# One core, one long program: the same steps in another order on every engine

## The chip, the cores and the metric

The kernel runs on one core of a Trainium2 chip. A core has engines with an instruction queue each, which run side by side and wait for one another by semaphores: TensorE (PE in the profile; PEld are its weight loads), VectorE (DVE), ScalarE (ACT), GpSimd (POOL) and SyncE (SP), which here issues all transfers between the chip's memory and the core's own memory (SBUF). TensorE writes its results to PSUM, eight banks of 2 KB per partition. The metric is the time of one run on the device, in microseconds (us), as the median of several runs; lower is better.

## The reference

A gated linear attention, computed token by token, is followed by a feed-forward block with a hard-swish.

```python
def _attn_ref(q, k, v, alpha):            # each (4, 8, 768, 48)
    state = np.zeros((B, H, D, D), dtype=np.float32)
    for t in range(S):
        state = alpha[:, :, t, :, None] * state + np.einsum('bhd,bhe->bhde', k[:, :, t], v[:, :, t])
        y[:, :, t] = np.einsum('bhd,bhde->bhe', q[:, :, t], state)

def _moe_ref(x, w_in, w_out):             # x (3072, 384), w_in (384, 2048), w_out (2048, 384)
    h = x @ w_in
    g = h * np.clip(h + 3.0, 0.0, 6.0) / 6.0
    return g @ w_out
```

x is the attention's output with batch and sequence as rows and heads times 48 as columns. The weights come as 64-bit floats and the kernel rounds them itself.

## The kernel before

The 3072 tokens are worked on as 24 chunks of 128 (index j), six for each of the four batch entries, and the feed-forward block as 12 groups of two chunks (index g). Everything is unrolled: the program is a list of 1788 words such as `ta.0.0`, and each word emits the few instructions of one step. The name ahead of the first point is the step, the numbers are the chunk or group, a part, and the buffer or PSUM bank that is used. As each engine runs its queue in order, the list is at the same time the order of every engine's queue, and of SyncE's transfers. No scheduler changes it (`tc.manual_schedule()`); the framework only puts in the semaphores.

The steps, by their names in the list, with the line that shows in the profile and the engine:

- Loads on SyncE: `la`, `lk`, `lq` bring alpha, k and q of a chunk (L251 for chunks 0 to 5, one transfer; L262 from chunk 6 on, four transfers into tiles in blocks of 32, with two small memsets on GpSimd, L257, for chunks 6 and 7). `lv` brings v in two halves (L272). `w.i` brings slice i of the weights (L162 for the eight slices of w_in, L166 for the eight of w_out) into one of five buffers, of which slices 0 and 5, 1 and 6, 2 and 7 and so on share one.
- Rounding a weight slice: ScalarE takes the low half (`d1`, L186), the magnitude (`d2`, L196) and, for slices 0, 1, 2 and 4, the sign (`dx`, L191, 1.9 us); VectorE puts the high bits together (`d3`, L203 and L205, or L207, L208 and L210); GpSimd adds both (`d4`, L217). Slice i of w_in is needed by block i of the first product, slices 8+2p and 9+2p of w_out by part p of `b`.
- Attention of a chunk: `ta`, `tk`, `tq` turn alpha, k and q on TensorE (L282) for chunks 0 to 5; later chunks are turned by VectorE (L286). `ca` copies alpha (L300, ScalarE), `r` scans it backwards and inverts (L309, L313), `p` scans it forwards (L320), `k` and `q` multiply by the scans (L332, all VectorE). `sc` makes the scores (L346, TensorE), `m` masks them (L356, VectorE), `qa` copies q (L366, ScalarE). `kb` turns k back (L374) and `ck` copies it (L378, ScalarE); from chunk 8 on `kt`, `kw`, `kr` do that by VectorE and two trips through memory. `u` updates the state (L429, TensorE), `sm` adds it (L437, L439, VectorE), `st` decays it (L409, GpSimd), `sv` copies it (L419, ScalarE; L415, a memset on GpSimd, at the start of a batch entry). `ya` and `yb` make the two halves of the output (L455, TensorE), `cy` copies it to x (L464, ScalarE).
- Feed-forward of groups 0 and 1: `fa`, `fb` (halves, L489) and `f` (L478) are the first product, `fr` (L494, ScalarE) and `fg` (L498, VectorE) the gate, `b` (L516) the second product for the two chunks of group 0, `bo` and `so` copy and store it.
- Feed-forward of groups 2 to 11: a fast bilinear scheme with 20 small products for 24. `y` (L537 to L541, VectorE) makes sums of weight blocks once, `xc` sums of x blocks for each group, `M.g.i` is product i (L600, TensorE), `n` copies some products (L606, ScalarE), `o` sums them (VectorE), `e` and `h` are the gate (L494, L498).
- Second product of groups 1 to 11, by a Strassen-like scheme: `x` (L647) sums weights once, `s` (L647, L664) sums the gated block (VectorE), `P.g.i` is product i (L703, TensorE), `K` and part 3 of `G` copy (L682, L716, ScalarE), the other `G` add (L719, VectorE), `O` stores (L724, SyncE). The four buffers of `G` are named by the last number.
- `z.m.n` is a filler: n matmuls of the identity into bank m (L532) that nobody reads.

The words begin with the fillers and the first chunk, and the step table and the loop that runs them are the whole control:

```python
    def run(words):
        for word in words.split():
            name, *at = word.split(".")
            steps[name](*(int(x) for x in at))
```

Of the kernel before, what the change touches and what calls it, by code (L numbers as in the profile page):

```python
# [17 lines left out]
def kernel(  # L18
# [42 lines left out]
    G = 2  # L61
# [510 lines left out]
    for i in range(8):  # L572
        r, o = divmod(i, 3)
        spots.append(raws[r].rearrange("p n w -> p (n w)").bitcast(FP)[:, o * QB : (o + 1) * QB])
    xc = consts.tile([C, len(X_SUMS), C], FP, tag="xc")
# [174 lines left out]
    with tc.manual_schedule():  # L750
        run("""z.0.5 z.0.3 z.0.1 z.0.8 qa.0.0 w.0 d2.0 d3.0 la.0 ta.0.0 ca.0 r.0 lk.0 tk.0.1 k.0
               z.0.2 p.0 la.1 ta.1.2 lq.0 tq.0.3 ca.1 r.1 lk.1 lv.0.0 sv.0.0 d1.0 kb.0.0 ck.0 z.0.2
               u.0.2.1 sm.0.0 sv.0.1 q.0 qa.0.1 tk.1.0 k.1 p.1 z.0.2 sc.0.2.3 m.0 la.2 ta.2.0 ca.2
               dx.0 w.2 d2.2 kb.1.0 ck.1 lq.1 r.2 sm.0.1 st.1 tq.1.2 q.1 d3.2 z.0.3 d1.2 dx.2 lv.1.1
               u.1.3.1 sv.1.0 sm.1.0 p.2 sm.1.1 sc.1.0.2 m.1 ya.0.3 yb.0 cy.0 lq.2 w.1 d1.1 tq.2.1
               q.2 d4.2 lk.2 tk.2.3 k.2 fa.2.0 d4.0 st.2 sc.2.0.2 d2.1 d3.1 m.2 dx.1 d4.1 qa.1.1
               lk.3 la.3 ta.3.1 ca.3 la.4 fa.0.1 sv.1.1 w.3 r.3 ta.4.3 ca.4 r.4 tk.3.1 k.3 kb.2.0
               qa.1.0 d2.3 ya.1.2 yb.1 cy.1 fa.1.2 lq.3 ck.2 d1.3 p.3 d3.3 lv.2.2 u.2.3.2 sm.2.0
               d4.3 fb.2 tq.3.1 q.3 fb.1 qa.2.0 sm.2.1 sv.2.0 st.3 fr.0.2.0 fg.0.2 lk.4 tk.4.0
               sv.2.1 w.5 d2.5 k.4 d3.5 d1.5 qa.3.0 d4.5 qa.2.1 sc.3.1.3 m.3 w.6 d2.6 d1.6 d3.6 d4.6  # L760
               lv.3.0 lq.4 w.7 kb.3.2 fb.0 f.0.3.3 kb.4.0 ya.2.1 ck.3 u.3.3.2 sm.3.0 fr.0.3.1 fg.0.3
               fr.0.1.0 fg.0.1 qa.3.1 sv.3.0 sm.3.1 p.4 d2.7 sv.3.1 d1.7 d3.7 d4.7 f.0.5.0 fr.0.5.1
               fr.0.0.0 fg.0.5 fg.0.0 tq.4.3 ck.4 la.5 ta.5.2 f.0.6.3 ca.5 w.4 d2.4 ya.3.0 yb.3 cy.3
               fr.0.6.1 yb.2 cy.2 w.9 d2.9 q.4 qa.4.1 d1.4 d1.9 dx.4 la.6 w.8 d3.4 r.5 lk.5 w.10
               d3.9 p.5 ca.6 fg.0.6 d4.9 w.12 lq.5 lv.4.1 d2.8 d3.8 f.0.7.2 d1.8 st.4 d4.8 d4.4 w.11
               fr.0.7.0 fg.0.7 f.1.7.0 fr.1.7.1 fg.1.7 sc.4.0.2 m.4 f.1.1.1 fr.1.1.0 fg.1.1 f.1.3.3
               fr.1.3.1 d2.10 d1.10 tk.5.3 f.1.0.2 d2.12 d3.10 d4.10 w.13 fg.1.3 fr.1.0.0 fg.1.0 k.5
               d3.12 lq.6 f.1.6.0 f.1.2.1 u.4.1.0 sm.4.0 d1.12 d4.12 sv.4.0 qa.4.0 ya.4.2 fr.1.6.1
               fg.1.6 w.15 tq.5.3 fa.4.3 sv.4.1 d2.11 kb.5.1 d2.13 fr.1.2.0 f.1.4.2 fr.1.4.1 d1.11
               sm.4.1 q.5 r.6 d3.11 d3.13 fg.1.4 d4.11 lv.5.0 lk.6 tq.6 p.6 d2.15 d3.15 fg.1.2 d1.13  # L770
               d4.13 sc.5.0.3 yb.4 f.1.5.0 fr.1.5.1 fg.1.5 tk.6 m.5 b.1.0.2 fb.4 b.1.1 d1.15 d4.15
               st.5 y.5 w.14 la.7 lk.7 cy.4 d2.14 qa.5.1 ck.5 b.0.0.1 fr.0.4.0 d3.14 k.6 q.6 ca.7
               fg.0.4 d1.14 d4.14 x.0 y.1 y.10 b.0.1 y.0 y.2 u.5.2 P.1.0.0 K.1.0 qa.5.0 sv.5.0
               qa.6.1 P.1.1.3 b.0.2 b.1.2 kb.6.0 ya.5.3 y.6 s.1.0.0 sm.5.0 sv.5.1 G.1.0.0 tk.7
               s.1.1.1 s.1.2.3 x.1 yb.5 cy.5 b.1.3 sc.6.1.2 lv.6.2 ck.6 u.6.3.0 s.1.3.2 x.2 P.1.2
               b.0.3 K.1.1 y.7 s.1.4 s.1.5 y.11 y.3 r.7 xc.2.1 x.3 y.4 y.8 xc.2.3 k.7 xc.2.0 xc.2.4
               y.9 y.12 y.16 y.13 y.15 P.1.3.3 K.1.2 P.1.4 bo.1 P.1.5 xc.2.5 G.1.1.1 P.1.6 y.14 y.17
               y.19 xc.2.6 sm.6.0 G.1.2.2 y.20 M.2.0.2 lv.12.1 la.8 O.1.1 O.1.0 ca.8 y.18 y.21 y.23
               so.1 G.1.3.3 n.2.0.8 bo.0 lq.7 lv.7.0 O.1.2 m.6 xc.2.2 xc.2.10 xc.2.7 tq.7 r.8 p.7
               xc.2.8 sv.6.1 M.2.15.3 M.2.1 kb.7.3 n.2.1.9 M.2.16 M.2.2 n.2.2.10 M.2.7.0 n.2.7.11  # L780
               sm.6.1 xc.2.9 q.7 p.8 M.2.3 M.2.4 n.2.4.12 M.2.8 o.2.0.0 M.2.5 n.2.5.13 qa.7.0 sv.6.0
               st.7 lk.8 O.1.3 lq.8 lk.9 la.9 la.10 tk.8 tq.8 lq.10 lq.9 ya.6.1 yb.6 M.2.9 z.1.3
               M.2.18.1 o.2.1.0 e.2.1.1 M.2.10 cy.6 ck.7 sc.7.0.2 u.7.1.3 n.2.10.14 M.2.11 qa.7.1
               ca.9 la.11 y.22 M.2.6.2 h.2.1 q.8 m.7 e.2.0.0 h.2.0 n.2.11.15 qa.6.0 n.2.18.10 qa.8.1
               M.2.12 M.2.19 n.2.12.12 M.2.13 sm.7.0 sv.7.1 r.9 k.8 o.2.3.0 sv.7.0 ya.7.0 y.24
               o.2.5.0 n.2.13.12 o.2.2.0 yb.7 cy.7 sc.8.1.2 xc.3.1 o.2.2.1 e.2.2.1 xc.3.3 o.2.3.1
               M.2.14 xc.3.4 xc.3.0 xc.3.5 o.2.4.0 xc.3.7 xc.3.6 o.2.6.0 P.2.0.1 M.3.0.2 M.2.17
               h.2.2 o.2.6.1 e.2.3.0 h.2.3 o.2.7.0 K.2.0 n.3.0.12 M.3.1 n.3.1.9 e.2.5.1 M.3.7.0
               n.3.7.13 xc.3.8 o.2.7.1 xc.3.2 kt.8 e.2.6.0 h.2.6 tk.9 M.3.2 n.3.2.10 e.2.4.0 P.2.1.3
               h.2.4 h.2.5 s.2.0.14 e.2.7.0 G.2.0.1 h.2.7 M.3.3 M.3.4 n.3.4.8 k.9 s.2.1.11 M.3.8  # L790
               o.3.0.0 ca.10 kt.9 P.2.3.3 s.2.2.15 s.2.3.14 lv.8.2 kw.8 kr.8 lk.10 sm.7.1 xc.3.9
               M.3.5 n.3.5.11 K.2.2 e.3.0.1 xc.3.10 M.3.9 o.3.1.0 P.2.2 K.2.1 u.8.0.3 M.3.18.2 s.2.5
               M.3.10 n.3.10.14 n.3.18.15 e.3.1.0 s.2.4 P.2.4 tq.9 h.3.0 st.8 sv.8.0 M.3.11 n.3.11.8
               tk.10 p.9 sm.8.0 q.9 r.10 k.10 qa.9.0 qa.9.1 m.8 sm.8.1 h.3.1 M.3.19 o.3.5.0 kt.10
               P.2.5 G.2.2.0 st.9 M.3.12 sc.9.0.1 qa.8.0 n.3.12.10 o.3.3.0 kw.9 lv.9.0 kr.9 sv.8.1
               u.9.2.3 sm.9.0 sv.9.1 sv.9.0 G.2.1.2 sm.9.1 st.10 M.3.15.2 M.3.16 M.3.6.3 M.3.13 m.9
               o.3.4.0 o.3.6.0 tq.10 n.3.13.10 o.3.2.0 e.3.4.1 ya.8.2 yb.8 ya.9.3 yb.9 cy.9 M.3.14
# [135 lines left out]
```

## Time and profile before

| | us |
|---|---|
| median of 3 runs | 535.52 (535.26 to 536.1) |
| the profiled execution | 535.44 |
| its span, first to last instruction | 533.7 |
| TensorE busy | 524.6 |
| VectorE busy | 477.2 |
| ScalarE busy | 257.2 |
| GpSimd busy | 50.4 |
| GpSimd's 16 steps `d4` (L217), 0 to 95 us | 26.9 |

Busy time is the union of an engine's instructions; an engine may be busy and yet not at its best pace, and TensorE's instructions overlap. In a row of the timeline the columns are start, duration, engine, line, operation, result and operands, how many instructions are merged, and in brackets the idle time ahead of it with the instruction that ended it. What the profile calls the chain that ended last gives TensorE 85% of the span and VectorE 8%, nearly all of the latter between 80 and 128 us.

### The profile page before, as it was taken

The numbers are of one execution on the slowest core, as the hardware profiler recorded it, in microseconds if no ns is written. First come the engines' busy times: TensorE is split into PE (matmuls) and PEld (weight loads), VectorE is DVE, ScalarE is ACT, GpSimd is POOL, SyncE is SP. The second block draws the span as 40 slices with busy tenths as digits, with TensorE's granted clock in tenths as the row PEclk, the third lists the DMA queues.
The fourth block names the chain that finished last, engine by engine and source line by source line (L and its number), as shares of the span: only waits on it lengthen the run. The fifth ranks groups of instructions, "written<-read, shape, count | busy, mean of one in ns | idle before, by whom it ended". The sixth has DMA issues, their size and how long they took to land.

```text
span 533.7 us, 15143 instructions
## 1 busy us (share of the span) xinstructions
PE 524.6 (98%) x6306; PEld 499.4 (94%) x6306; DVE 477.2 (89%) x849; ACT 257.2 (48%) x503; POOL 50.4 (9%) x71
## 2 busy tenths in 40 slices
PE   8799999999999999999999999999999999999997
PEld 7698886789999999999999999999999999999997
DVE  6999989999999999998999999999999899496382
ACT  3889865212653553553544444642634544553340
POOL 5333425100000000000000000000000000000000
DMA  9998876005615155254344355044454042100001
GB/s 174 217 252 256 215 216 152 21 2 154 152 30 116 32 121 135 57 140 95 87 110 113 91 124 140 19 120 102 115 136 104 11 110 43 44 2 2 15 16 37
DMA packets 124100, 54.40 MB, mean 102 GB/s; under 512 B 83328, under 2 KB 116864, under 8 KB 124032
## 3 DMA queue, kind: packets, MB, share of 16 engines
q1 hardware_dynamic: 124032, 53.44, 42.5%
q8 instruction: 49, 0.80, 0.6%
q14 instruction: 19, 0.16, 0.1%
HBM read 44.50 MB, written 8.91 MB: 100 GB/s over the span
## 4 chain that ended last, share of the span: by engine, by line
PE 85%; DVE 8%; POOL 2%; DMA 2%; ACT 1%; issue 1%; SPq 1%; DVEq 0%; POOLq 0%
PE m_ps L703 34%; PE m_ps L600 34%; PE m_ps L478 5%; PE t_ps L455 4%; PE t_ps L346 2%; PE t_ps L429 2%; PE m_ps L489 2%; PE t_ps L282 1%; DVE rings L647 1%; DMA v<-in_v_dram 1%; DVE raw L537 1%; ACT raw L191 1%; DMA kq<-in_k_dram 1%; DVE g_sb L647 1%; DVE w L537 1%
## 5 line engine op out<-in xcount | busy, mean ns | idle before, releaser
L606 ACT COPY g_sb<-m_ps 128x512 f32<-128x512 f32 x110 | 63.6, 584 | 124.9 <-PE m_ps L600 104.1
L703 PE MATMUL m_ps<-w,g_sb 128*128 128x192 f32 x704 | 121.7, 327 | 0.0
L703 PEld LDWEIGHTS m_ps<-w,g_sb 128*128 128x128 f32 x704 | 113.7, 190 | 0.4
L703 PE MATMUL m_ps<-rings,g_sb 128*128 128x192 f32 x528 | 91.5, 326 | 0.0
L703 PEld LDWEIGHTS m_ps<-rings,g_sb 128*128 128x128 f32 x528 | 85.4, 190 | 0.1
L600 PE MATMUL m_ps<-xc,w 128*128 128x128 f32 x640 | 82.7, 277 | 0.3 <-DVE w L541 0.3
L600 PEld LDWEIGHTS m_ps<-xc,w 128*128 128x128 f32 x640 | 77.5, 192 | 1.5 <-issue 0.5
L494 ACT ACTIVATE r<-g_sb,half 128x512 f32<-128x512 f32 x80 | 56.8, 722 | 32.9 <-DVE g_sb L541 12.1
L498 DVE SCALAR_TENSOR_TENSOR g_sb<-r,g_sb 128x512 f32<-128x512 f32 x80 | 53.6, 682 | 4.6 <-ACT r L494 4.2
L600 PE MATMUL m_ps<-xT,raw 128*128 128x128 f32 x400 | 52.5, 277 | 0.0
L600 PEld LDWEIGHTS m_ps<-xT,raw 128*128 128x128 f32 x400 | 48.6, 192 | 0.6
L409 POOL TENSOR_TENSOR st<-sm,R 128x192 f32<-128x192 f32 x20 | 12.9, 643 | 353.8 <-DVE sm L439 306.7
L647 DVE TENSOR_TENSOR g_sb<-g_sb 128x512 f32<-128x512 f32 (+1 forms) x55 | 42.0, 795 | 0.2
L600 PE MATMUL m_ps<-xT,w 128*128 128x128 f32 x320 | 42.0, 276 | 0.0
L600 PEld LDWEIGHTS m_ps<-xT,w 128*128 128x128 f32 x320 | 39.3, 192 | 0.1
L366 ACT COPY A<-q 48x256 f32<-48x256 f32 x88 | 35.5, 404 | 5.0 <-DVE q L332 3.7
L356 DVE TENSOR_TENSOR A<-t_ps,mask 64x256 f32<-64x256 f32 x96 | 36.0, 414 | 0.4
L478 PE MATMUL m_ps<-xT,w 128*128 128x256 f32 x144 | 32.8, 382 | 0.0
L600 PE MATMUL m_ps<-xc,raw 128*128 128x128 f32 x240 | 31.8, 276 | 0.0
L309 DVE TENSOR_TENSOR_SCAN R<-t,ones 128x516 f32<-128x516 f32 x24 | 29.7, 1236 | 1.1 <-ACT t L300 1.0
L478 PEld LDWEIGHTS m_ps<-xT,w 128*128 128x128 f32 x144 | 26.7, 190 | 3.6
L600 PEld LDWEIGHTS m_ps<-xc,raw 128*128 128x128 f32 x240 | 29.6, 192 | 0.1
(104 smaller groups left out, 731.0 us busy)
## 6 DMA issues: line engine op xcount, KB each, us to landing
raw<-in_moe_w_out_dram SPq DMA_DIRECT2D x8, 768.0 KB, 5.2
raw<-in_moe_w_in_dram SPq DMA_DIRECT2D x6, 768.0 KB, 6.8
v<-in_v_dram SPq DMA_DIRECT2D x48, 96.0 KB, 3.0
out_dram<-oh SPq DMA_DIRECT2D x44, 96.0 KB, 1.7
far<-kq SPq DMA_DIRECT2D x64, 64.0 KB, 2.2
kb<-far SPq DMA_DIRECT2D x64, 64.0 KB, 2.0
aq<-in_alpha_dram SPq DMA_DIRECT2D x36, 96.0 KB, 2.5
qq<-in_q_dram SPq DMA_DIRECT2D x36, 96.0 KB, 2.4
```

The source lines that it names most:

```text
L309: nc.vector.tensor_tensor_scan(out=reverse(R, n - 1, n), data0=reverse(ax, n, n), data1=reverse(ones, n, n), initial=0.0, op0=ALU.mult, op ...
L356: nc.vector.tensor_tensor(out=to[:, a], in0=sc[a][half], in1=mask[half, half].unsqueeze(1).to_broadcast([HB, NP, HB]), op=ALU.mult)
L366: nc.scalar.copy(out=to[:, a], in_=Q_t[j][64 * a : 64 * a + D, :, half])
L409: nc.gpsimd.tensor_tensor(out=st, in0=sm, in1=R_t[j][:, :, 0:1].to_broadcast([C, NP, D]), op=ALU.mult)
L455: nc.tensor.matmul(y_of(j, (i + 1) // 2, p)[:, HB * b : HB * b + HB], vb[:, p, e : e + 32], A_t[j][:, b, 2 * p + a], start=(b == 0 and i = ...
L478: nc.tensor.matmul(h[:, f], w1[:, kk, o : o + C], xT_t[g][:, kk], start=(kk == 0), stop=(kk == KT - 1))
L494: nc.scalar.activation(out=to, in_=h, func=AF.Relu, bias=half, scale=1.0 / 6.0)
L498: nc.vector.scalar_tensor_tensor(out=to, in0=r, scalar=1.0, in1=h, op0=ALU.min, op1=ALU.mult)
L600: nc.tensor.matmul(acc[g][i][:, f * C : (f + 1) * C], spots[w][:, f * C : (f + 1) * C], x_of(g, x), start=(first and f == 0), stop=last, s ...
L606: nc.scalar.copy(out=slots[z], in_=acc[g][i])
L647: nc.vector.tensor_tensor(out=out, in0=in0, in1=in1, op=ALU.subtract)
L703: nc.tensor.matmul(to[g], a, rhs[:, f], start=(first and f == 0), stop=(last and f == HF - 1), skip_group_check=True)
```

## The change

The list of words is replaced by another one. It holds the same 1788 steps, each once as before; what differs is their order, the PSUM bank or buffer that a step is given, and how the 29 fillers are split. Nothing else in the file changes. The change is described as an order searched anew on a model in which, of GpSimd and VectorE, the first comer takes the lock that they share. Core of the diff:

```diff
-        run("""z.0.5 z.0.3 z.0.1 z.0.8 qa.0.0 w.0 d2.0 d3.0 la.0 ta.0.0 ca.0 r.0 lk.0 tk.0.1 k.0
-               z.0.2 p.0 la.1 ta.1.2 lq.0 tq.0.3 ca.1 r.1 lk.1 lv.0.0 sv.0.0 d1.0 kb.0.0 ck.0 z.0.2
-               u.0.2.1 sm.0.0 sv.0.1 q.0 qa.0.1 tk.1.0 k.1 p.1 z.0.2 sc.0.2.3 m.0 la.2 ta.2.0 ca.2
-               dx.0 w.2 d2.2 kb.1.0 ck.1 lq.1 r.2 sm.0.1 st.1 tq.1.2 q.1 d3.2 z.0.3 d1.2 dx.2 lv.1.1
-               u.1.3.1 sv.1.0 sm.1.0 p.2 sm.1.1 sc.1.0.2 m.1 ya.0.3 yb.0 cy.0 lq.2 w.1 d1.1 tq.2.1
-               q.2 d4.2 lk.2 tk.2.3 k.2 fa.2.0 d4.0 st.2 sc.2.0.2 d2.1 d3.1 m.2 dx.1 d4.1 qa.1.1
...
-               xc.2.8 sv.6.1 M.2.15.3 M.2.1 kb.7.3 n.2.1.9 M.2.16 M.2.2 n.2.2.10 M.2.7.0 n.2.7.11
...
-               st.7 lk.8 O.1.3 lq.8 lk.9 la.9 la.10 tk.8 tq.8 lq.10 lq.9 ya.6.1 yb.6 M.2.9 z.1.3
...
-               e.11.2.0 h.11.2 s.11.4 e.11.3.1 h.11.3 P.11.1.0 G.11.0.2 s.11.5 O.11.0 K.11.1 P.11.4
-               G.11.1.0 P.11.5 G.11.2.1 O.11.2 P.11.6 G.11.3.2 O.11.1 O.9.2 O.11.3""")
+        run("""z.0.8 qa.0.0 w.2 z.0.3 z.0.2 la.0 ta.0.0 z.0.3 d2.2 d3.2 d1.2 ca.0 lk.0 tk.0.1 r.0
+               k.0 la.1 p.0 dx.2 z.0.5 ta.1.2 ca.1 r.1 lq.0 tq.0.3 q.0 p.1 lv.0.0 kb.0.0 z.0.2 ck.0
+               w.0 u.0.1.2 z.0.2 sm.0.0 sc.0.0.3 m.0 lq.1 tq.1.1 q.1 sm.0.1 lk.1 tk.1.0 k.1 sc.1.1.3
+               d1.0 d2.0 d3.0 dx.0 qa.0.1 m.1 sv.0.1 w.1 d2.1 d3.1 z.0.3 kb.1.2 d1.1 ck.1 la.2
+               ta.2.0 ca.2 d4.2 sv.0.0 ya.0.1 lk.2 tk.2.3 r.2 k.2 p.2 dx.1 la.3 ta.3.2 z.0.1 yb.0
+               cy.0 ca.3 st.1 r.3 qa.1.1 qa.1.0 kb.2.0 ck.2 lv.1.1 u.1.3.1 sm.1.0 lq.2 tq.2.2 q.2
+               p.3 d4.0 fa.0.0 fa.2.1 w.5 d2.5 d3.5 sc.2.0.3 m.2 sv.1.0 ya.1.2 sv.1.1 yb.1 d1.5 cy.1
...
+               sc.4.2.3 st.4 d1.12 d4.12 f.1.7.1 f.1.6.3 f.1.3.2 fr.1.3.0 fg.1.2 k.5 lk.6 w.11 d2.11
+               lq.7 lv.4.1 m.4 fg.1.3 d3.11 f.1.1.0 fr.1.1.1 fg.1.1 d1.11 d4.11 lq.5 fr.1.6.0 fg.1.6
+               tk.6 w.13 d2.13 d1.13 d3.13 b.0.0.2 b.0.1 u.4.0.1 sm.4.0 fr.1.7.1 fg.1.7 lk.7 lv.5.0
...
+               y.23 G.1.2.3 n.2.0.8 M.2.1 M.2.15.0 n.2.1.9 M.2.2 q.7 tk.7 lk.8 tk.8 r.8 xc.2.8
...
+               qa.7.1 M.2.16 M.2.3 M.2.4 M.2.8 k.7 kb.7.2 M.2.18.2 o.2.4.0 sm.6.1 st.7 n.2.4.12
...
+               o.11.2.1 e.11.2.0 h.11.2 s.11.4 K.11.1 K.11.2 h.11.3 P.11.1.2 s.11.5 P.11.4 G.11.1.2
+               G.11.0.0 O.11.0 P.11.5 P.11.6 O.10.2 O.11.1 O.10.1 G.11.3.0 G.11.2.3 O.11.2 O.11.3""")
```

## The prediction

> **What bounds the kernel now.** I read the page's first lines, then busy time by stretches, then every gap in the timeline of TensorE, then VectorE beside GpSimd. Times are microseconds (us) of the profiled execution.
>
> ```profile
> span 533.7 us, 15143 instructions
> PE 524.6 (98%) x6306; PEld 499.4 (94%) x6306; DVE 477.2 (89%) x849; ACT 257.2 (48%) x503; POOL 50.4 (9%) x71
> ...
> 20.00:40.00 20.00, 18.55 (x395) 16.77 (x396) 19.64 (x34) 18.40 (x30) 8.85 (x7) 1.00 1.04 225
> 40.00:60.00 20.00, 20.00 (x276) 17.14 (x275) 19.56 (x31) 19.40 (x33) 7.55 (x7) 1.00 0.79 234
> 60.00:80.00 20.00, 20.00 (x222) 17.33 (x221) 18.23 (x32) 13.46 (x22) 7.17 (x8) 1.00 0.85 225
> 80.00:100.00 20.00, 20.00 (x104) 15.06 (x103) 19.73 (x26) 9.42 (x18) 8.58 (x14) 1.00 0.50 115
> 100.00:130.00 30.00, 29.71 (x277) 24.80 (x276) 29.84 (x53) 5.26 (x13) 0.00 (x0) 1.00 0.18 48
> 130.00:200.00 70.00, 70.00 (x954) 68.39 (x956) 67.89 (x126) 36.94 (x76) 2.92 (x4) 1.00 0.41 95
> ```
>
> The columns of the stretches are PE, PEld, DVE, ACT, POOL, granted clock, DMA share, GB/s. TensorE is busy without a hole from about 31 us to its end at 530.8, but for 0.3 us in 100 to 130. Start to start its matmuls keep one pace for each shape: 0.112 us at 128 columns, 0.163 at 192, 0.216 at 256, 0.323 at 384, 0.109 for a turn (L282, L374). So TensorE sets the end, and only two things can move it: where its steady work begins, and where VectorE, itself 98% busy from 20 to 130, hands something over too late. Beginning, one late handover, a filler and one collision look like this:
>
> ```profile
> 1.46 6.75 PE L532 MATMUL m_ps<-ident 128*128 128x128 f32 x34 [1.46 <-POOL ident masks.py:199]
> ...
> 24.90 1.60 PE L489 MATMUL m_ps<-xT,w 128*128 128x128 f32 x12 [0.25 <-POOL w L217]
> ...
> 126.69 1.06 PE L600 MATMUL m_ps<-xT,raw 128*128 128x128 f32 x8
> 128.04 1.13 PE L600 MATMUL m_ps<-xc,w 128*128 128x128 f32 x8 [0.29 <-DVE w L541]
> ...
> 137.91 0.83 PE L532 MATMUL m_ps<-ident 128*128 128x128 f32 x6
> ...
> 92.19 0.68 DVE L332 TENSOR_TENSOR k<-k,R 128x512 f32<-128x512 f32 x1
> 92.51 1.69 POOL L217 TENSOR_TENSOR w<-raw 128x768 int32<-128x768 int32 x1 [3.76 <-DVE raw L210]
> 92.80 1.95 DVE L332 TENSOR_TENSOR q<-q,P 128x512 f32<-128x512 f32 x1
> ```
>
> The first product of the feed-forward part starts at 24.90. At 128.04 TensorE waits for VectorE (step y.23); against its pace it loses 0.45 there. Six filler matmuls lie amid useful work at 137.91. The last lines are the lock of the change's title: GpSimd is in an L217 from 92.51 to 94.20; a VectorE product that takes 0.68 by itself starts at 92.80 and ends at 94.75, so it sat behind GpSimd for 1.27.
>
> **The change, part by part.** Both orders hold the same 1788 steps, the same counts of instructions on each engine and 29 fillers each (58 matmul rows). Nothing is added or removed, so each cost is one of place.
>
> Useful work of TensorE: big products 1600 x 0.1116 + 1232 x 0.1626 + 144 x 0.2157 + 96 x 0.1116 + 64 x 0.3227 + 104 turns x 0.109 = 452.7. The 3008 small products (L346, L429, L455) stand in 43 separate stretches now and 44 after. A stretch costs about 0.3 beside its products: 32 rows of L455 take 0.58, 64 take 1.03, so 0.13 is paid for each group, and 0.09 and 0.10 more are lost at the change of shape before and behind. Term: +0.3, bounds 0 and +0.6.
>
> The beginning. Loads go through one queue in order. Counted by packets in the trace, a load of k, q, v or alpha (1024 packets of 192 bytes) takes 1.2, a weight slice (384 of 2 KB) 2.35, the first data moves at 2.0, and an engine sees it about 1.2 after the last packet (v.0: packets end 11.9, landing 13.13). The new queue is w.2, la.0, lk.0, la.1, lq.0, lv.0, w.0, lq.1, lk.1, w.1, la.2, lk.2, la.3, lv.1, lq.2. Added up, they can be used at: w.0 14.2, w.1 18.9, la.2 20.1, lk.2 21.3, lv.1 23.7, lq.2 24.9. Two more weight slices now stand ahead of la.2 than did, and all of w.0's and w.1's rounding with it. ScalarE in its new order, with 0.93 for each of L186 and L196 and 1.93 for L191: w.0's three steps and the copies 14.2 to 19.5, w.1's two to 21.4, kb.1's copy 22.0, ca.2 22.6, w.1's sign (dx.1) 24.5, cy.0 25.0, ca.3 25.6, the q copies 27.2. VectorE: r.2 behind ca.2 ends 24.2 (1.22 + 0.18), k.2 24.9, p.2 26.1, r.3 27.5, q.2 28.6. TensorE: kb.2 behind k.2, u.1, tq.2 (lq.2 is there by then), so fa.0, the first product, starts at 26.5, where fa.2 starts at 24.90 now. But more has been done by then. Ahead of it now: 44 turns x 0.109, six small groups (3.5) in three stretches (0.2 each beyond the groups) = 8.9. After: 52 turns, six groups (3.6) in six stretches = 10.4. The shortfall, clock minus work done, is 16.0 now, and 16.3 once the 0.30 gap at 30.3 (ahead of ya.1, behind ScalarE) is in; after, 16.1. Term: -0.2. Its bounds: if w.0 were seen as soon as its last packet lands (1.2 earlier) the ScalarE row moves whole: -1.4; if each of w.0, la.2 and lq.2 queues 0.6 longer: +1.6.
>
> The clock. The first 26 filler rows run 0.213 apart until 6.96, the later ones 0.111. The new order has just 26 filler rows ahead of ta.0, so ta.0's four turns could meet the slow pace: 4 x 0.11 = 0.44 later for r.0, which waits less than fa.0's loads do, so 0 in the sum. [...]
>
> The filler. z.1.3 (six rows x 0.111 = 0.67) stands at 137.91 now; in the new order all fillers stand ahead of fa.0. What covers it now is the wait that would follow: M.2.8, a few steps earlier, ran 0.36 behind VectorE. Term: -0.67 if TensorE is the bound there, 0 if VectorE is.
>
> VectorE. I set, for each product, VectorE's work up to the instruction that it needs (durations of this trace, 0.06 off each since neighbours overlap) against TensorE's work ahead of the product. The larger the difference, the tighter. Now the tightest of 100 to 130 of TensorE's work is M.2.1 on y.23, 5.6 (it waits); after it is kb.7 on k.7, 6.5. In 130 to 140 it is 6.8 now (P.2.1, with 0.44 to spare) and 7.2 after. Later: 7.1 and 6.9 near 177, 4.7 (1.45 to spare) and 5.4 near 217, 4.2 and 4.5 near 245. So the new order leans on VectorE a little harder. Against that VectorE starts earlier: ta.0 has 13 fillers ahead of it, not 17, and q.2 ends 7.7 behind VectorE's own work, where it ended 8.4 behind (25.60 on the clock). Shift at P.2.1: 7.2 - 6.8 - 0.44 - 0.7 = -0.7; TensorE's own there would be -0.2 - 0.67 - 0.45 = -1.3. The later one counts: -0.7.
>
> Collisions. Five VectorE instructions below 100 us stretch beside GpSimd: 0.28, 0.41, 0.40, 1.17 and 1.27 over their usual time, 3.5 in all. The sums above carry them along, on the same steps. After, the sixteen L217 (24 us of GpSimd) meet other instructions. With none, VectorE's shift is -0.7 - 3.2 and TensorE's own -1.3 stands; with twice as many, +2.8. I take as many as now, as the rows of the same kinds of instruction are all that is left to meet: 0.
>
> The end. P.11.6 and a copy by ScalarE close both orders (0.32, then the store, 2.5). Three more stores (O.10.2, O.11.1, O.10.1) wait behind O.11.0, which is ready two products (5.2) before the end, so they cost nothing; were O.11.0 late by more than that, each would add an issue of about 0.6.
>
> Other moves past queues: w.11 stands behind lk.6 on SyncE and needs the buffer of w.8's d4. By VectorE's place of d3.8 that is free at 60, so the slice is seen at 65.5, ahead of d3.11's turn at 70, and d4.11 ends about 74 where b.0.1 comes at 74.9. That cover is 1 us; if it were gone, b.0.1 and ScalarE behind d2.11 would stall by what is missing. The stores standing ahead of loads later leave 10 us of TensorE's work at the closest (kr.20; now 8.5 for kr.22).
>
> **Sum.** -0.7 from the later of the two engines; the extra stretch lies where VectorE is the bound and is covered. Span 533.0. The profiled execution took 535.44, its span 533.66, so 1.8 lies around it; the median of the runs is 535.52, 0.08 above. Forecast 535.52 - 0.7 = 534.8.
>
> **The rivals.**
> Fewer collisions: VectorE keeps ahead and TensorE's own terms stand, -1.3, with the start at its lower bound -2.5: 533.0 to 534.2. For it: 3.2 of stretched instructions are there to be saved below 130. Against it: VectorE is then the bound nowhere, and nothing more can be gained than the beginning.
> VectorE is caught worse: an L217 lies 1.47 long, and two more hits on instructions like that of 92.80 (1.27 each) than now, between 20 and 130. VectorE is the later engine there, so all of it passes on: -0.7 + 2.5 = +1.8, 537.3, slower. Half a hit more eats the gain; from one and a half on ((0.7 + 1.07) / 1.27) it is slower by more than 0.2%. For it: the new order is tighter on VectorE, 6.5 for 5.6. Against it: five hits in 110 us show that most L217 meet nothing.
> The beginning is late: la.2, lk.2, lv.1 and lq.2 all stand behind three weight slices, where one or two stood. If lq.2 comes at 27 instead of 24.9, tq.2 and fa.0 wait for it: +1.6, 537.1. For it: DMA is at its limit below 26 us (share 1.16 and 1.04). Against it: the queue is in order and its pace even.
> The order not coming out as written can be left aside: the built instructions stand as the text has them.
>
> **How the numbers follow.** Forecast 0.45 (534.8, its own range 533.9 to 536.0), fewer collisions 0.20 (533.6), VectorE caught 0.20 (537.3), late beginning 0.15 (536.9). I call 0.2% (1.07 us) what a measurement of this kernel tells from no change: faster is below 534.45, slower above 536.59. Faster: 0.15 of the forecast and all 0.20 of the second. Slower: 0.03 of the forecast, 0.16 and 0.09 of the others: 0.28. The rest, 0.37, is within. Range 532.9 to 537.8: it leaves out the lower tip of the second and the upper parts of the last two.
>
> **What would show it.** Fillers all below 20 us, and the first L489 near 26.5. The share of TensorE from 31 on unchanged; the wait for VectorE near 128 (y.23, k.7) at 0 to 0.9. L207, L309 and L332 rows over their usual 0.55, 1.22 and 0.68 where L217 runs: how much above 3.5 in all is the second against the third case. It is wrong if TensorE shows a hole of a microsecond or more behind 31, at b.0.1 above all, or starts its products later than 28.

## The result, and the profile after

| | old order | new order |
|---|---|---|
| median | 535.39 (535.25 to 536.1, 4 runs) | 541.0 (540.69 to 542.63, 4 runs) |
| ratio to the old order, 95% interval | | 1.0106, 1.0094 to 1.0118 |
| profiled execution, its span | 535.44, 533.7 | 540.69, 538.9 |
| VectorE busy | 477.2 | 484.3 |

The new order is 5.6 us slower. The forecast was 534.8 with a range up to 537.8, so it is wrong in sign and outside its range. The first lines of the page and the stretches of the new order, to be held against those of the old one:

```profile
span 538.9 us, 15119 instructions
PE 526.6 (98%) x6306; PEld 500.9 (93%) x6306; DVE 484.3 (90%) x849; ACT 257.6 (48%) x503; POOL 48.5 (9%) x71
...
PEclk9699999999999999999999999999999999999999
```

```profile
20.00:40.00 20.00, 19.65 (x327) 18.08 (x321) 19.00 (x29) 15.55 (x26) 5.86 (x4) 0.87 1.01 242
40.00:60.00 20.00, 18.80 (x312) 16.41 (x311) 19.61 (x30) 16.09 (x30) 6.68 (x10) 1.00 0.83 209
60.00:80.00 20.00, 18.11 (x109) 14.48 (x108) 19.53 (x29) 12.94 (x17) 8.07 (x10) 1.00 1.00 234
...
100.00:130.00 30.00, 29.25 (x340) 25.25 (x339) 29.83 (x46) 3.81 (x10) 0.00 (x0) 1.00 0.01 2
```

Three things differ. VectorE is busy for 7.1 us more with the same instructions. TensorE has holes in 40 to 80 (18.80 and 18.11 of 20, where it had 20.00). And the granted clock shows 0.87 in 20 to 40, where it was 1.00.

The prediction's measure, clock minus useful work of TensorE, tells where the time went. Here it is at equal amounts of work done, in us, each matmul at its shape's pace and fillers at nothing; the last column is an experiment told below:

| useful work done | old order | new order | new order, additions cut, fillers added |
|---|---|---|---|
| 10 | 17.07 | 19.73 | 17.26 |
| 26 | 18.53 | 21.35 | 17.71 |
| 50 | 19.04 | 24.70 | 18.22 |
| 80 | 20.17 | 25.96 | 19.20 |
| 105 | 20.51 | 27.51 | 19.71 |
| end | 27.65 | 32.91 | 25.98 |

The new order loses 2.7 before its first products, 3.0 more up to 50 of work (75 us on the clock) and 1.3 up to 105, and then gains 1.7. The next lines, from the timeline of the new order (engines put together by time), show the largest of the losses:

```profile
10.15 1.85 POOL L217 TENSOR_TENSOR w<-w,raw 128x768 int32<-128x768 int32 x1 [3.15 <-ACT raw L191]
10.21 2.88 DVE L320 TENSOR_TENSOR_SCAN P<-t 128x516 f32<-128x516 f32 x1
...
26.58 1.85 POOL L217 TENSOR_TENSOR w<-w,raw 128x768 int32<-128x768 int32 x1 [3.73 <-ACT raw L191]
26.75 2.77 DVE L320 TENSOR_TENSOR_SCAN P<-t 128x516 f32<-128x516 f32 x1
28.68 2.84 PE L489 MATMUL m_ps<-xT,w 128*128 128x128 f32 x24
...
39.29 1.47 POOL L217 TENSOR_TENSOR w<-g_sb 128x768 int32<-128x768 int32 x1 [2.42 <-ACT r L494]
39.46 0.68 DVE L498 SCALAR_TENSOR_TENSOR g_sb<-r,m_ps 128x512 f32<-128x512 f32 x1
40.06 0.68 DVE L332 TENSOR_TENSOR q<-t_ps,P 128x512 f32<-128x512 f32 x1
...
68.97 1.84 POOL L217 TENSOR_TENSOR w<-w,g_sb 128x768 int32<-128x768 int32 x1 [4.30 <-ACT w L196]
69.34 1.89 DVE L207 TENSOR_SCALAR w<-w 128x768 f32<-128x768 f32 x1
70.77 1.78 POOL L217 TENSOR_TENSOR w<-raw 128x768 int32<-128x768 int32 x1
71.27 1.71 DVE L208 TENSOR_SCALAR w<-w 128x768 uint32<-128x768 uint32 x1
74.08 0.68 DVE L498 SCALAR_TENSOR_TENSOR g_sb<-r,m_ps 128x512 f32<-128x512 f32 x1
74.81 2.86 PE L478 MATMUL m_ps<-xT,w 128*128 128x256 f32 x12 [1.89 <-DVE g_sb L498]
```

GpSimd's d4.2 begins at 10.15, VectorE's scan p.0 comes 0.06 later, and takes 2.88 where it takes 1.22 alone. The same befalls p.2 at 26.75. Between them stands a harmless meeting: the L498 and L332 of 39.46 and 40.06 also run beside an L217, but read PSUM (`m_ps`, `t_ps`), and take their usual 0.68. At 69 two additions in a row, d4.4 and d4.10, stretch both halves of d3.12; behind it on VectorE stands fg.1.2 (L498 at 74.08), whose input from ScalarE was there at 69.3, and behind that TensorE, for 1.89. In all, seven VectorE rows are longer by 0.8 or more: p.0 1.66, p.2 1.55, r.4 0.93, p.5 0.83, d3.12 1.32 and 1.14, y.2 1.14 against the old order; 8.6 in sum. Against the new order the old one has three rows of 0.40 or more: 0.40, 1.11 and 1.27. (The other two of the prediction's five, 0.28 and 0.41 over their usual time, are L203 rows that are longer in the new order too, by 0.22 and 0.29; the first runs beside a memset of GpSimd and not beside an L217.)

The clock and a third kind of loss, first the granted clock by stretches of the new order, then two rows of TensorE's timeline, then the instruction queue's line of the transfers from 108 to 110 us:

```profile
14.00:16.00 2.00, 0.94 (x32) 0.94 (x32) 1.93 (x4) 1.94 (x3) 0.00 (x0) 0.74 1.18 189
16.00:20.00 4.00, 2.81 (x32) 1.84 (x29) 3.96 (x10) 3.34 (x6) 0.51 (x1) 0.50 1.03 236
...
24.00:26.00 2.00, 2.00 (x42) 1.83 (x42) 1.42 (x3) 1.95 (x2) 0.00 (x0) 0.70 0.80 225
```

```profile
109.02 1.10 PE L455 MATMUL t_ps<-A,v 128*32 128x64 f32 x61
110.87 0.30 PE L455 MATMUL t_ps<-A,v 128*32 128x64 f32 x3 [0.75 <-issue]
```

```profile
q8 instruction: 1, 0.02, 4.0%
```

The clock is at 0.50 from 15.0 to 25.2: turns go 0.213 apart there instead of 0.109. At 110 TensorE stands still for 0.75 in the middle of a row of equal small products, waiting for nothing that the profile shows. In that stretch one packet of the instruction queue was under way (108.33 to 109.61); that it brings TensorE's instructions is a guess, with its grounds below. A like wait, 0.51, ends at 54.45 in the row ya.2, ya.3, yb.3, yb.2.

### The profile page after: what moved, and what is told of

The parts are those of the page before. It is cut to its first block, busy times and chain, and to the rows that moved or that the text cites. A ratio compares the mean times of both kernels' runs of the same rounds, so it can differ in the third digit from the quotient of the medians.

```text
span 538.9 us, 15119 instructions
## 1 busy us (share of the span) xinstructions
PE 526.6 (98%) x6306; PEld 500.9 (93%) x6306; DVE 484.3 (90%) x849; ACT 257.6 (48%) x503; POOL 48.5 (9%) x71
## 4 chain that ended last, share of the span: by engine, by line
PE 86%; DVE 8%; DMA 3%; issue 1%; SPq 1%; ACT 0%; POOL 0%; POOLq 0%
PE m_ps L703 37%; PE m_ps L600 34%; PE m_ps L516 4%; PE t_ps L455 4%; PE t_ps L346 2%; PE t_ps L429 2%; DVE R L309 1%; PE m_ps L478 1%; DVE P L320 1%; DMA raw<-in_moe_w_out_dram 1%; DMA raw<-in_moe_w_in_dram 1%; DVE A L356 1%; DMA v<-in_v_dram 1%; DVE w L208 1%; DVE k L332 1%
## 5 line engine op out<-in xcount | busy, mean ns | idle before, releaser
L498 DVE SCALAR_TENSOR_TENSOR g_sb<-r,g_sb 128x512 f32<-128x512 f32 x80 | 54.2, 685 | 3.8 <-ACT r L494 3.1
L600 PE MATMUL m_ps<-xT,raw 128*128 128x128 f32 x400 | 51.3, 276 | 0.0
L320 DVE TENSOR_TENSOR_SCAN P<-t 128x516 f32<-128x516 f32 x24 | 33.3, 1389 | 0.1
L478 PEld LDWEIGHTS m_ps<-xT,w 128*128 128x128 f32 x144 | 26.7, 190 | 5.9 <-DVE g_sb L498 2.3
L537 DVE TENSOR_TENSOR g_sb<-g_sb 128x512 f32<-128x512 f32 x40 | 26.9, 684 | 5.4 <-ACT g_sb L606 5.3
```

Source lines behind the costliest of these rows:

```text
L320: nc.vector.tensor_tensor_scan(out=P_t[j], data0=aX[j % 2][:, 0:n], data1=ini[j % 2], initial=0.0, op0=ALU.mult, op1=ALU.add)
L478: nc.tensor.matmul(h[:, f], w1[:, kk, o : o + C], xT_t[g][:, kk], start=(kk == 0), stop=(kk == KT - 1))
L498: nc.vector.scalar_tensor_tensor(out=to, in0=r, scalar=1.0, in1=h, op0=ALU.min, op1=ALU.mult)
L537: eng.tensor_tensor(out=out, in0=in0, in1=in1, op=ALU.add if s1 > 0 else ALU.subtract)
L600: nc.tensor.matmul(acc[g][i][:, f * C : (f + 1) * C], spots[w][:, f * C : (f + 1) * C], x_of(g, x), start=(first and f == 0), stop=last, s ...
```

## The experiments

Three theories stood against each other: L, the additions stretch VectorE; C, the clock; O, the order hands things over late by itself.

### No additions in the way, in both orders

```diff
         high = dst if i in BY_HALVES else hi
+        if True:
+            dst, high, lo = (x[:, 0:1, 0:8] for x in (dst, high, lo))
```

> The new order with GpSimd's sixteen additions (d4, L217) cut from 768 columns to 8, so most of a rounded weight's low part is left out. Theory L (lock): in the new order nine VectorE instructions that read and write SBUF alone start while an L217 runs and are stretched by 9.0 us in all (2.8 in the old order); with the additions gone these rows are back at their usual length and the time falls by 5 to 7, to 534 to 536. Theory C (clock): TensorE's granted clock falls to 0.50 from 15.0 to 25.2 us; that stays, so the time falls by less than 2.5, to 538.5 to 541. Theory O (the order hands over late by itself, whatever GpSimd does): 540 to 541, with the 1.9 us hole ahead of f.1.1 at 72.9 still there.

> The old order with the same cut of the sixteen additions. Theory L: only 2.8 us of stretched VectorE rows go (at 29.4, 82.5 and 92.8), of which TensorE feels what lies ahead of its 0.45 wait at 128: the time falls by 0.5 to 2.5, to 533 to 535, and the gap between the two orders shrinks from 5.6 to between 0 and 2. Theory C: the gap stays at 4 or more. Theory O: the gap stays at 5 to 6.

The new order: 537.25 (535.88 to 539.93, 11 runs), ratio 1.0028 (1.0011 to 1.0044). The old one: 535.0 (534.84 to 536.08), ratio 0.9993 (0.9984 to 1.0001). The gap shrinks from 5.6 to 2.25, where L had at most 2, C 4 or more and O 5 to 6; the 537.25 itself lies between L's 536 and C's 538.5. Part of what remained was told by the runs themselves: those of the new order fall into groups by their mean granted clock, 535.88 to 536.12 at 0.996 to 1.000, 537.25 to 538.22 at 0.994, 539.64 and 539.93 at 0.990. One kernel, one list, and of what the runs list only the clock differs. So L holds for the larger part, and beside it C.

### The clock

More fillers, in two versions (in the profile each of the n of a filler z.m.n shows as two matmuls); the first also delays p.0, as its eight matmuls ahead of `ta.0` come ahead of that turn on TensorE:

```diff
+ z.0.4   (ahead of ta.0.0, first version only)
+ z.0.1   (ahead of tq.0.3, first version only)
+ z.0.6   (ahead of sc.0.0.3; z.0.4 in the second)
+ z.0.3   (ahead of tq.1.1; z.0.2 in the second)
+ z.0.5   (ahead of sc.1.1.3; z.0.4 in the second)
```

> The new order with 38 filler matmuls more in TensorE's holes below 20 us (8 ahead of ta.0, 2 ahead of tq.0, 12 ahead of sc.0, 6 ahead of tq.1, 10 ahead of sc.1), so that the clock has no reason to fall. Theory C: the clock stays at 1.00, the turns at 16 to 25 us run 0.11 apart instead of 0.21, the first L489 starts 1.5 to 2.2 earlier than 28.68, and the time falls by 1.2 to 2.5 to 538.5 to 539.8. Theory L: VectorE, busy without a gap from 6.6 to 24.1, is the later engine, so at most the 0.54 gap at 24.1 comes back: 540.3 to 541. If the clock doesn't depend on the fillers: clock still 0.50 and 541 to 542.

> The new order with fillers only inside waits that TensorE has anyway, none ahead of ta.0: 8 matmuls ahead of sc.0, 4 ahead of tq.1, 8 ahead of sc.1. The first trial's 8 ahead of ta.0 had put p.0 from 10.21 to 11.10. Theory C (clock is a part of its own): clock 1.00 below 30, first L489 near 27.2, time 538.5 to 540. Theory L (in the beginning VectorE is the later engine, the slow clock is covered): first L489 at 28.2 to 28.7, 540.3 to 541.

The first gave 540.28 (539.26 to 541.01), the second 541.1 (540.84 to 542.42). A stretch of the second one's trace, and two rows of its timeline:

```profile
20.00:24.00 4.00, 3.92 (x87) 3.56 (x88) 3.89 (x8) 3.30 (x5) 1.85 (x1) 1.00 0.76 146
```

```profile
10.52 2.90 DVE L320 TENSOR_TENSOR_SCAN P<-t 128x516 f32<-128x516 f32 x1
...
28.71 1.70 PE L489 MATMUL m_ps<-xT,w 128*128 128x128 f32 x7
```

From 12 to 26 the clock is now 1.00, the scan is hit as before, and the first product begins at 28.71, where it began at 28.68; at 26 of work the shortfall is 21.44, where it was 21.35. With the hits in place, VectorE's lateness covers the slow clock of the beginning: there C falls as a part of its own. It isn't cleared wholly. In the new order VectorE had one wait there for a copy of what the slow TensorE had turned, 0.54 ahead of r.2 at 24.67; it is gone here, but p.0 starts 0.31 later in this execution, and the clock still fell once, later (0.74 in 26 to 30).

The same with the additions cut, where nothing covers it, and the opposite for the old order, four filler words fewer:

```diff
+ z.0.3   (new order, additions cut: ahead of tq.1.1)
+ z.0.4   (ahead of sc.1.1.3)
- z.0.2   (old order: behind k.0; behind ck.0; behind p.1)
- z.0.3   (old order: behind d3.2)
```

> The new order with the additions cut to 8 columns, and 6 fillers ahead of tq.1 and 8 ahead of sc.1. Eleven runs without these fillers fell into three groups by granted clock: 535.9 to 536.1 at 0.996 to 1.000, 537.3 to 538.2 at 0.994, 539.6 to 539.9 at 0.990. Theory C: the fillers leave only the first group: median 535.9, none above 536.6; what is then left over the old order without additions (535.0) is the order's own, 0.9. If the groups have another cause than the clock: median 537 as before, spread to 539.9.

> The old order with four filler words left out (18 matmuls: behind k.0, behind ck.0, ahead of sc.0, behind d3.2, at 8.9, 11.9, 14.3 and 18.2 us), nothing else. If a thin beginning makes the clock fall whatever the order: turns 0.21 apart somewhere from 14 to 25, mean clock 0.99 to 0.997, first L489 1 to 3 later than 24.90, time 536.5 to 539. If the old order doesn't need them: clock 1.00 and 535.2 to 535.9.

The new order without additions now takes 534.25 (533.75 to 534.4, 6 runs, clock 0.999 to 1.000), ratio 0.9971 (0.996 to 0.9983): under the old order, and 1.6 lower than I expected of it. Its scans and its first product:

```profile
10.29 1.24 DVE L320 TENSOR_TENSOR_SCAN P<-t 128x516 f32<-128x516 f32 x1
...
26.20 2.84 PE L489 MATMUL m_ps<-xT,w 128*128 128x128 f32 x24
```

So O falls: without the additions, and with the clock kept up, the order is no worse than the old one (535.0 without additions). The 3.0 to the kernel without fillers are not the clock alone, as theory C had it; I had expected 535.9, what that kernel gave at clock 1.000. Between the two profiled executions (537.49 and 533.75) 1.36 of the 3.74 is there at 10 of work, where the clock was 0.50 from 17.6 to 24.4 in the first and 1.00 in the second, and most of the rest comes at two places, 51 and 107 us, by waits that a later part takes up. In the old order the thinner fillers make it fall as well, and cost 1.05: 536.73 (536.18 to 537.53, clock 0.987 to 0.994), ratio 1.0021 (1.0012 to 1.003). Its trace from 16 to 20:

```profile
16.00:20.00 4.00, 2.53 (x11) 1.73 (x9) 3.91 (x9) 3.38 (x4) 0.27 (x1) 0.50 1.30 226
```

### Only the additions that hit, and only the others

> The new order with only six of the sixteen additions cut to 8 columns: d4.2, d4.1, d4.7, d4.9, d4.4 and d4.10, those that ran when VectorE came to p.0, p.2, r.4, p.5 and d3.12; with the 6 and 8 fillers ahead of tq.1 and sc.1. Theory L: these six are all that counts, so it comes to what all sixteen gave (534.25): 534.2 to 535.0 (the hit on y.2 at 96 stays and costs nothing). If GpSimd's work as such slows VectorE, wherever it lies: 537 to 538.5.

> The counterpart: the other ten additions cut to 8 columns, the six left whole; fillers as in the second trial with fillers (541.1). Theory L: 540.3 to 541.2, nothing gained. If GpSimd's work as such slows VectorE: 537.5 to 539.

Six cut: 535.23 (eight of eleven runs 534.85 to 535.3, the others to 537.17), a little over L's 535.0. Ten cut: 539.4 (538.93 to 539.4 in the three runs at clock 1.000, 540.55 and 541.09 at 0.996 and 0.997), 1.7 under the 541.1 where L had nothing gained: a miss, for the ten weren't wholly free. By far the larger part still lies with the six. So GpSimd's work as such isn't the matter, its place is. The sizes are read best from the shortfall at 130 of work, at clock 1.00 and ahead of a wait at 187 us that has another cause: 20.52 with all sixteen cut, 21.32 with six cut, 25.22 with ten cut. Six additions whole cost 4.7, ten whole 0.8.

### The whole computation, with steps moved

```diff
@@ ScalarE: d4.2 becomes ready later
-la.1 p.0 dx.2 z.0.5
+la.1 p.0 z.0.5
...
-z.0.2 ck.0 w.0
+z.0.2 ck.0 dx.2 w.0
@@ VectorE: fg.1.2 ahead of d3.12
-fg.1.0 d2.12 d3.12 f.1.2.0
+fg.1.0 k.5 d2.12 f.1.2.0
...
-fr.1.3.0 fg.1.2 k.5 lk.6
+fr.1.3.0 fg.1.2 d3.12 d4.12 lk.6
```

> The new order with three steps moved, same operations: ScalarE's dx.2 behind ck.0, so that d4.2 no longer runs when VectorE comes to p.0; and VectorE's d3.12 (with d4.12) behind fg.1.2, k.5 ahead of it. Theory L: p.0 (L320) takes 1.22 instead of 2.88, and f.1.1 no longer waits 1.9 for fg.1.2, which stood behind the stretched d3.12 while its input was there at 69.3: the time falls by 1.5 to 3.5, to 537.5 to 539.5. Theory C: p.0 alone changes little while the clock is at 0.50: 540 to 541. Theory O: about 539 (only the hole at 72.9 goes).

> The kernel with the three moved steps (dx.2, d3.12, k.5), and 6 fillers ahead of tq.1 and 8 ahead of sc.1. Moved alone gave 536.75 at clock 1.000 and 537.9 to 538.3 at 0.993. Theory C: 536.5 to 537.0 in nearly all runs, clock 0.997 or more. If the slow clock is covered by VectorE: no change, 537.5 to 538.3.

Moved alone: 537.93 (536.75 to 538.32), 3.1 less than the new order. With fillers 537.14 (536.56 to 537.49, clock 1.000 in all ten runs), ratio 1.0024 (1.0015 to 1.0033). From the timeline of the first:

```profile
10.20 1.22 DVE L320 TENSOR_TENSOR_SCAN P<-t 128x516 f32<-128x516 f32 x1
...
26.37 2.84 PE L489 MATMUL m_ps<-xT,w 128*128 128x128 f32 x24
...
67.39 0.68 DVE L498 SCALAR_TENSOR_TENSOR g_sb<-r,m_ps 128x512 f32<-128x512 f32 x1
```

One ScalarE step put 4 us later (dx.2 starts at 12.17, not 8.13) frees p.0; k.2, which the steps ahead of the first product wait for, ends 2.3 earlier (24.55, not 26.83), and so does the first product. fg.1.2 runs at 67.39, ahead of the stretched d3.12, and f.1.1 no longer waits. What is left over 534.25 in the kernel with fillers is 2.9; its trace still has p.2 (1.09), r.4 (0.93), p.5 (0.83), the second half of d3.12 (1.14) and y.2 (1.14) stretched. So I moved r.4, p.5 and d3.12 out of the way:

```diff
-sm.2.1 m.3 w.7 d2.7 d3.7
+sm.2.1 w.7 d2.7 d3.7 m.3
-q.4 p.5 fg.0.6
+q.4 fg.0.6 sm.3.1 p.5
-fg.1.2 d3.12 d4.12
+fg.1.2 m.4 d3.12
-d4.11 lq.5
+d4.11 d4.12 lq.5
```

> Whole computation. The kernel with three moved steps and the fillers (537.14), and further steps moved so that VectorE has instructions that read PSUM, or none that is hit, while GpSimd adds: m.3 behind d3.7; fg.0.6 and sm.3.1 ahead of p.5; m.4 ahead of d3.12; d4.12 behind d4.11. Left: the hit on p.2 (1.1). Theory L: r.4, p.5 and d3.12 lose 0.93, 0.83 and 1.14 of stretch, 537.1 - 2.0 to 2.9 = 534.2 to 535.2, below the old order's 535.7. If moved steps bring new waits: 536 to 537.5.

537.68 (536.67 to 538.6): a miss. r.4, p.5 and d3.12 were free of hits, but d3.7 and d3.13 took new ones (0.69 and 0.90), that on p.2 grew to 1.45, and TensorE, against its pace, lost 0.98, 1.61 and 1.00 at 35, 52 and 187 us to waits that nothing in the profile released.

### Waits that nothing released

In these traces such a wait inside or just behind a row of small products ends after a packet of the instruction queue has landed, 1.1 to 1.3 after it in the five named here: in the new order the packets land at 53.20 and 109.61, TensorE goes on at 54.45 and 110.87; without additions 52.22 and 106.35, and 53.55 and 107.69. The old order has one such wait too, 0.95 up to 20.00, after a packet that lands at 18.93, but none behind 31. The first of the latter, from that timeline (its line numbers are two higher):

```profile
49.98 1.64 PE L457 MATMUL t_ps<-A,v 128*32 128x64 f32 x99
53.55 0.64 PE L457 MATMUL t_ps<-A,v 128*32 128x64 f32 x29 [1.93 <-issue]
```

These two waits, 1.93 and 0.80, are gone in the kernel with fourteen filler matmuls more, and one of 0.61 is there at 183 instead. If the theory that follows is right, every matmul added ahead of a row moves that row against the ends of the packets, so a filler does more here than keep the clock up (0.999 to 1.000 with the fourteen, 0.990 to 1.000 without). The page counts 49 such packets of 16 KB, and 50 with the fourteen more. TensorE passes 6306 matmuls and as many weight loads; if all these packets are TensorE's, one holds some 257 instructions (an estimate, 12612 / 49). A row of 128 small products with their weight loads, 256 instructions, takes 2 us (1.99 at 180.93 in the kernel with the fourteen). One packet was seen to go by the count of instructions and not by the clock: it lands at 109.61 in the new order and at 106.35 without additions, and sets out in both when TensorE has begun 2311 of the instructions in its trace. Theory F, a guess from these counts, is that TensorE runs out of instructions where such a row meets the end of a packet (the block of the expectations below). It was tried by splitting such rows:

```diff
-yb.9 cy.9 o.3.4.0 M.3.6.2 cy.8
+o.3.4.0 M.3.6.2 yb.9 cy.9 cy.8
@@ whole computation only
-ya.2.0 ya.3.1 yb.3 yb.2 cy.2 cy.3
+ya.2.0 yb.2 cy.2
...
+f.0.7.3 ya.3.1 yb.3 cy.3
```

> The new order with all additions cut to 8 columns and the 6 and 8 fillers (534.25; its trace had one wait of TensorE that nothing in the profile released, 0.77 at 183.1 us, in a row of 160 small products). Here yb.9 and cy.9 stand behind M.3.6, so that the row is 128 long. Theory F (TensorE runs out of instructions when a row of small products, 250 instructions in some 2 us, meets the end of a fetched block): no such wait at 183, 533.4 to 533.8. If the wait has another cause: still there, 534.2 to 534.5.

> Whole computation. The kernel with three moved steps and fillers (537.14; unreleased wait of 0.96 at 186.0), with yb.9 and cy.9 behind M.3.6, and the row ya.2, ya.3, yb.3, yb.2 split: ya.2 and yb.2 stay, ya.3, yb.3 and cy.3 stand behind f.0.7. Theory F: the wait at 186 goes, 536.0 to 536.5. Otherwise 537.0 to 537.4.

> Whole computation. The last kernel with fg.0.5 behind fg.0.3 (in place of m.3 behind d3.7), fg.0.6 and sm.3.1 ahead of p.5, m.4 ahead of d3.12, d4.12 behind d4.11. The first such kernel (537.68) had lost the stretches of r.4, p.5 and d3.12, but its trace has unreleased waits of 0.98, 1.61 and 1.00 at 35.1, 51.8 and 187.2 that ate them. Theory L with F: those at 51.8 and 187.2 go, 534.2 to 535.6. If the moved steps cost by themselves: 536.5 to 538.

Without additions: 533.88 (533.41 to 534.2), against 534.25 unsplit. The place in both traces, first unsplit, then split:

```profile
183.95 1.83 PE L600 MATMUL m_ps<-xc,w 128*128 128x128 f32 x14 [0.61 <-issue]
```

```profile
182.22 1.16 PE L600 MATMUL m_ps<-xc,w 128*128 128x128 f32 x8
183.30 1.06 PE L455 MATMUL t_ps<-A,v 128*32 128x64 f32 x32
```

The wait of 0.61 is gone, and the medians differ by 0.37, nearly as F had it (533.4 to 533.8); the spreads of the two overlap. The other two kernels were spoilt by my edit, 540.7 and 542.88: cy.3 had come to stand on ScalarE behind d1.10, whose slice lands at 58.3, and TensorE's tk.5 waited 4.0 for cy.3 to give its bank free. Mended, by putting f.0.7, ya.3, yb.3 and cy.3 ahead of w.10:

> Whole computation. The split kernel of the last trial had a wait of its own: cy.3 stood on ScalarE behind d1.10, whose slice came from memory at 58.3, and tk.5 waited 4.0 for cy.3's bank. Here f.0.7, ya.3, yb.3 and cy.3 stand ahead of w.10 and d1.10; else the same. Theory F: no wait at 51 or 186, 536.0 to 536.6 (against 537.14 unsplit). Otherwise 537.0 to 537.5.

> Whole computation. That kernel with fg.0.5 behind fg.0.3, fg.0.6 and sm.3.1 ahead of p.5, m.4 ahead of d3.12, d4.12 behind d4.11, so that r.4, p.5 and d3.12 meet no addition, or a short rest of one. Theory L with F: 534.2 to 535.6, level with the old order or under it. If the moved steps cost by themselves: 536.5 to 538.

536.6 (536.42 to 537.43), ratio 1.0023 (1.0013 to 1.0033), 0.54 less than unsplit, and no wait at 186. F holds there for the wait; the time doesn't show it, since the spreads overlap and the split brought two waits of its own, 0.62 that nothing released at 36 and 1.10 for cy.3 at 56.95, while two for VectorE (0.43 and 0.90 at 62 and 74) went. The last one gave 537.37 (537.13 to 537.87): the hits on d3.12 are gone and those on r.4 and p.5 shrunk to 0.33 and 0.09, but d3.13 takes a hit of 1.02, and TensorE still waits 1.07 for cy.3, up to 56.72. Freeing one row put another in the way. No version of the whole computation came under the old order.

### The filler at 137.91

```diff
-tk.8 tq.8 lq.10 lq.9 ya.6.1 yb.6 M.2.9 z.1.3
+tk.8 tq.8 lq.10 lq.9 ya.6.1 yb.6 M.2.9
```

> The old order without its filler z.1.3 (six matmuls at 137.91), the term of the prediction's sum that it tests. If TensorE is the bound there: 0.67 less, 534.9 to 535.1. If VectorE is (M.2.8, a few steps earlier, ran 0.36 behind it): 535.3 to 535.7.

535.34 (535.09 to 535.87), ratio 0.9997 (0.9989 to 1.0006): nothing. Its trace has a new wait for VectorE in the filler's place, 0.40 up to 139.61.

## Why the prediction was wrong, by its own steps

**The collisions, put at 0: the step that failed.** "I take as many as now" stood on "the rows of the same kinds of instruction are all that is left to meet", and the rival with more was held back by "most L217 meet nothing". Neither settles how many meet: that is set by the order. In the new one seven rows were hit for 8.6, against three for 2.8. By the cuts the six additions behind six of these rows are worth 4.7, the other ten 0.8; in the old order all sixteen are worth 0.7 (535.7 to 535.0, the medians of one session). The rival "VectorE is caught worse" named this mechanism, its engine and, but for the hit on p.0 at 10.21, its place; it priced two more hits of 1.27 where four more rows, and longer ones, came: seven of 0.83 to 1.66 for three. The additions of the slices rounded by halves last 1.85 and not 1.47. It deserved more than 0.20. The trace of before could have told which rows to look for: there, too, every VectorE row with a PSUM operand kept its length beside an L217 (42 rows, none more than 0.02 longer), and the stretched ones had none. With that, each d4 could have been followed to the row that VectorE reaches when dx or d3 has made it ready; dx.2 stands right behind p.0 in the new list.

**The beginning, -0.2.** Its loads and handovers were right: w.0 is taken up at 14.06 (I had 14.2), w.1 at 19.54 (18.9), and the first product comes at 26.1 to 26.7 in ten kernels in which p.0 is free, for 26.5 forecast (27.56 in the eleventh, without additions or added fillers, where the clock fell). In the new order it came at 28.68, since p.0 was hit and k.2 stands behind it on VectorE; p.2, hit at 26.75, comes behind k.2 and delays only what follows. The shortfall there grew by 2.7.

**The clock, 0.** It fell, and in this order that was covered but for at most the 0.54 that VectorE waited at 24.67, as the trial with fillers shows. But I had weighed only that ta.0's turns could meet the slow pace of the first fillers, not a fall behind them. It decides as soon as VectorE is on time, in runs of one and the same kernel: with the additions cut 1.1 to 2.3 at a mean of 0.994 and some 3.8 at 0.990; with three steps moved 1.2 to 1.6 (536.75 at 1.000, 537.93 to 538.32 at 0.993 and 0.994).

**The filler, -0.67 or 0.** It is 0: the wait that I named as its cover was there. The sum went by VectorE at that place, so nothing changed by it. The wait that came in its place was 0.40.

**VectorE harder to keep up with, -0.7.** In 100 to 130 TensorE waits for VectorE no more (29.25 of 30, and the missing 0.75 is the unreleased wait), where the prediction had a wait of 0 to 0.9, and from 105 of work to the end the new order gains 1.7. So far this part held; which engine is the later one there no run with the hits in place shows. With hits and clock out of the way the kernel ran in 534.25, and 533.88 with a row split, between the forecast's 534.8 and its rival with fewer collisions, 533.6.

**The stretches of small products, +0.3.** I counted stretches and not their length. The unreleased waits, which theory F puts down to that length, are missing from the sum: 0.51 and 0.75 in the new order behind 31 us, none in the old one. Why none of the old order's rows of 128 met a landing packet isn't shown; their places differ.

**b.0.1 and the end.** No hole there. The hole that I had warned of came a few steps earlier, at f.1.1, and not from w.11 but from d3.12.

Two slips of the sums change nothing: VectorE's "98%" from 20 to 130 is 97% by the rows shown (107.0 of 110), and the late beginning stands with 537.1 among the rivals and 536.9 among the chances.

What stays open is an exact division of the 5.6. An estimate from the measured parts: hits 4.7 + 0.8, less the old order's own 0.7; unreleased waits 0.5 + 0.75; the order's own gain, 533.88 - 535.0 = -1.1 (with seven fillers more and a row split). That makes 5.0. For the other 0.6 the clock and the way these losses cover each other are left, and no run parts them.

## What to carry to other kernels

When an order changes, list for every instruction of GpSimd what VectorE comes to in that time, and ask of each whether it reads PSUM. Those that did kept their length here (35 rows in the new order, none more than 0.02 longer); most of those that didn't, block transposes aside, waited for GpSimd to end (p.0 took 2.88 instead of 1.22), and the next in VectorE's queue waited with them. Three steps moved for this won back 3.1 us of 5.6; moving five more won nothing, as each row that was freed put another in the way. In this kernel VectorE's lateness hid another loss: with the hits in place, fillers that held the clock at 1.00 from 12 to 26 us gained nothing (541.1 for 541.0), and with the additions cut the runs at 0.994 and 0.990 were 1.1 to 3.8 longer than those at 0.996 to 1.000. Such causes don't add up one by one here.

## What the runs showed of the hardware

**Who is stretched.** In the new order 35 VectorE instructions with a PSUM operand ran beside an L217, and none was more than 0.02 longer than usual; nor was a block transpose (L286) by more than 0.04. Scans and products with two operands in SBUF (L309, L320, L332 of later chunks, L537) and L203, L207 and L208, where they started while an L217 ran, waited: as long as both overlap, less 0.13 to 0.15. It goes both ways: where VectorE's scan comes first, as in the kernel with three steps moved, d4.2 takes 2.04 instead of 1.85; in the old order the L217 of 81.81, behind the scan of 81.39, takes 2.02 instead of 1.46.

**The granted clock.** Where it fell, it stood at 0.50 for 3.41 us with three steps moved (19.03 to 22.44), for 6.8 with the additions cut (17.6 to 24.4) and for 10.24 in the new order (14.98 to 25.22). In the new order TensorE was busy for 1.81 of the 3.4 us from 11.6 to 15.0, and the clock fell at 15.0; without the additions it was busy for 1.48 from 14.2 to 17.6, and it fell there. In the old order 2.24 from 17.3 to 20.7 did not make it fall, nor did 1.64 from 23.9 to 27.3 in the first version with more fillers; so how busy TensorE is by these rows does not alone decide. The same kernel fell in some runs and not in others (with three steps moved, means of 0.993 and of 1.000).

**Waits in rows of small products.** In rows of 128 small matmuls TensorE stood still for 0.51 and 0.75 us in the new order and for 1.93 and 0.80 without additions, with nothing in the profile that released it. That it ran out of instructions there, theory F, is not shown. What speaks for F is the time of landing, the count of instructions and the waits that went when their rows were split (0.61 at 183 without additions, and the one at 186 with three steps moved).
